# A pooled-attention and gated-MLP kernel: two softmax groups of the first batch move a product to GpSimd, PSUM tiles and the opening order are reassigned

## The chip, the cores and the metric

The kernel runs on one core of one Trainium2 chip. The metric is the device time of one execution, in microseconds (us), as the median of several runs. Smaller is better.

Five instruction streams work side by side: PE (TensorE, the matmuls; its weight loads are listed as PEld), DVE (VectorE), ACT (ScalarE), POOL (GpSimd) and SP (SyncE, which here issues nearly all DMAs). Each carries out its own instructions strictly in the order in which they were written; a wait of one instruction holds up everything behind it on that engine.

## The reference

Inputs are `q`, `k`, `v` of shape 8 batches x 8 heads x 576 positions x 64 features in float32, and the weights of a gated MLP; `w_in`, `w_sg` (float32) and `w_out` among them. `w_in` and `w_out` come as float64.

```python
k_p = k.reshape(B, H, 72, 8, 64).mean(axis=3)     # pool 576 keys to 72
v_p = v.reshape(B, H, 72, 8, 64).mean(axis=3)
scores = q @ k_p^T / 8;  scores -= max(scores)
attn = exp(scores);  attn = attn / (sum(attn) + 1e-9)
x = attn @ v_p                                    # 8 x 576 x 512
h = gelu(x @ w_in);  u, v = h[..., :512], h[..., 512:]
v_n = (v - mean(v)) / sqrt(var(v) + 1e-6) * g_ln
v_s = einsum('ts,bsd->btd', w_sg, v_n) + b_sg
out = x + (u * v_s) @ w_out
```

The product of the change is the division by the row sum: `attn / (sum + 1e-9)`, done as a multiplication by a reciprocal.

## The kernel before

One batch after another runs through the same steps, and the instructions of several batches are interleaved by hand. Every step is a Python generator that emits some instructions and stops at each `yield`; the piece between two yields is called a phase here. Two lists of tokens say in which order the phases are emitted: PROLOGUE once, then PERIOD for each batch. A token such as `S0+1` runs the next phase of step S for group 0 of batch 1; a lower-case token such as `v0` runs the next phase of a weight step, and `lv0` loads weights. At the end of the program every instruction gets a dependency on the one before it on its engine, so the order of the tokens is the order on every engine and on the DMA queue of SP.

The steps: A and B load keys and values (two loads each, 2 groups of heads at once), C loads queries, E loads the last 8 pooled rows' raw data ("left"), K pools the keys (for batch 0 with matmuls into PSUM, `pool8`; later with a DVE reduction) and builds the transposed, scaled `kbd`; its own three phases for K2 are the DVE reduction of the left rows into `lp`, the transposes on PE, and four copies on ACT. P does the same for the values. Q makes the transposed queries (batch 0 on PE and ACT, later on DVE). S computes scores and softmax of one pair of heads ("group", 0 to 3). L and T transpose the probabilities, V multiplies by the values and writes x and its split into a high and a low float32r part. H, U, W, O are the MLP: the normalised half, the gate half, the product with w_sg, the output product. Z stores. The weight steps v, u, o convert a quarter of w_in or w_out from float64 words in five phases (two ACT, two DVE, one POOL, one ACT, one POOL instruction); the steps s transpose w_sg.

Step S (line 426) of batch 0 takes a PSUM tile from `mtile()`, of later batches from `atile()` (line 428). The groups listed in SOFTMAX (line 75), that is groups 0 and 3 of batch 0 and all of batch 1, go one way ("mode 2"): the maximum on DVE (line 439), scores minus maximum on DVE from PSUM to the tile `e` in SBUF (line 449), one exp on ACT (line 451), the row sum on DVE (line 459), plus 1e-9 on POOL (line 461). All other groups have 10 pairs of ACT instructions that take exp with the bias and accumulate the sum (line 456). Then the reciprocal goes into unused columns of the PSUM tile of the scores, and DVE multiplies:

```python
rec = flat[:, 0:SLOT * NT].rearrange(...)[:, :, 2 * SP:2 * SP + 2]
nc.vector.reciprocal(rec, ssum)
nc.vector.tensor_tensor(e, e, rec..., op=ALU.mult)
```

The last phase copies the columns of the left rows to the tile `el` on POOL (line 475), which step L transposes.

PSUM has room for four such tiles of two banks. They form two rings of two: `mps` from `mtile()` (line 93) and `aps` from `atile()` (line 96). Each call takes the other tile of its ring, and the first instruction that writes it waits until every reader of its last content is done.

Of the kernel before, what the change touches and what calls it, by code (L numbers as in the profile page):

```python
# [33 lines left out]
o1 K1+2 T1+1 T1+1 o1 o1 o0 W3+0 V0+1 B1+2 o1 o0 W2+0 T2+1 o0 V1+1 W3+0 T2+1 o3 o3 T2+1 o2 W0+0 V2+1 o2 K2+2 B0+2 o2
V1+1 T3+1 W1+0 T3+1 o3 T3+1 V1+1 W0+0 V2+1 Q0+2 W2+0 V2+1 W3+0 K2+2 W0+0 K2+2 W1+0 V3+1 V3+1 S0+2 W1+0 W0+0 Q1+2 P1+2
W2+0 W1+0 o2 S1+2 W3+0 S0+2 C2+2 P0+2 S0+2 V0+1 S1+2 Q2+2 O1+0 S1+2 C3+2 O1+0 O1+0 O0+0 O0+0 o2 V3+1 V3+1 O2+0 S0+2
O0+0 S2+2 o3 Z0+0 O2+0 S2+2 P2+2 H2+1 o3 S1+2 O2+0 A0+3 S2+2 C0+3 Z1+0 H2+1 T0+2 S0+2 Q3+2 A1+3 Z0+0 V1+1
# [760 lines left out]
```

## Time and profile before

| | before |
|---|---|
| median of 3 runs | 576.03 us (572.07 to 578.5) |
| the profiled execution | 574.59 us |
| its span, first to last instruction | 572.8 us |
| PE busy | 552.7 us, 96% of the span |
| DVE, ACT, POOL busy | 71%, 61%, 39% |
| mean granted TensorE clock | 0.993 of full speed (2.4 GHz) |

The span is what the trace covers; the 1.8 us between it and the execution's time lie around it. PE's busy share is high from the third of 40 slices to the last, so idle time of the other engines is to be read together with what PE waits for. In a row of a timeline the columns are: start in us, duration in us, engine, line, operation, output tile <- input tiles, shapes, count of merged instructions, and in brackets the idle time of the engine just before and what ended it.

### The profile page before, as it was taken

Reading aid. Unit: us, or ns where it says so; the run is one execution under the profiler, and the core shown is the slowest. Engines: PE = TensorE matmul, PEld = TensorE weight load, DVE = VectorE, ACT = ScalarE, POOL = GpSimd, SP = SyncE. Lnnn points to the kernel's source line nnn. Section 1 sums busy time; section 2 is a strip of 40 time slices with the busy share of each in tenths; the row PEclk is TensorE's granted clock in tenths of the full one; section 3 lists DMA queues with packets and bytes.
Section 4 is the critical chain, followed back from the end, with each engine's and each line's share of the span. In section 5 each row is a group of like instructions: output and inputs, shape, how many; then the busy total and the mean of one; then the engine's idle time right before and its main releaser. Section 6 shows DMA issues by size and latency. Waiting matters only on the chain.

```text
span 572.8 us, 10342 instructions
## 1 busy us (share of the span) xinstructions
PE 552.7 (96%) x3793; PEld 522.3 (91%) x3793; DVE 406.6 (71%) x572; ACT 350.9 (61%) x985; POOL 222.3 (39%) x304
## 2 busy tenths in 40 slices
PE   4699999999999999999999999999999999999996
PEld 4678899988999999998999989999999989998996
DVE  2688999978568875878667785778667765344454
ACT  1889795977549755677647766498546775412320
POOL 3437755933153340703335331523316231433240
PEclk9799999999999999999999999999999999999999
DMA  8996263452513435153411625133440211021105
GB/s 215 319 270 153 59 151 93 95 105 57 97 33 78 69 73 104 38 104 69 93 31 47 113 57 108 48 77 48 95 79 1 44 22 21 1 42 22 21 1 84
DMA packets 161602, 46.34 MB, mean 81 GB/s; under 512 B 149072, under 2 KB 149072, under 8 KB 161552
## 3 DMA queue, kind: packets, MB, share of 16 engines
q1 hardware_dynamic: 156688, 45.10, 36.6%
q10 hardware_dynamic: 4864, 0.59, 0.6%
q8 instruction: 30, 0.49, 0.4%
q14 instruction: 20, 0.16, 0.1%
HBM read 36.23 MB, written 9.44 MB: 80 GB/s over the span
## 4 chain that ended last, share of the span: by engine, by line
PE 83%; DVE 7%; DMA 4%; SPq 3%; ACT 2%; issue 1%; POOL 0%; DVEq 0%; ACTq 0%; POOLq 0%
PE mps L100 66%; PE aps L100 13%; PE aps L135 3%; SPq L155 3%; DMA stage<-in_moe_w_sg 1%; DMA qraw<-in_q 1%; DMA kvraw<-in_k 1%; DVE bst L583 1%; DVE nmax L439 1%; DVE e L469 1%; DVE e L449 1%; ACT e L456 1%; DVE vp L324 1%; DVE vg L589 0%; DVE ssum L459 0%
## 5 line engine op out<-in xcount | busy, mean ns | idle before, releaser
L100 PE MATMUL mps<-xhl,wih 128*128 128x288 f32 x512 | 89.9, 298 | 0.0
L100 PE MATMUL mps<-wih,xhl 128*128 128x512 f32 x256 | 85.7, 401 | 0.1
L100 PEld LDWEIGHTS mps<-xhl,wih 128*128 128x128 f32 x512 | 75.8, 188 | 1.7 <-ACT u L616 0.2
L671 POOL TENSOR_TENSOR glo<-u,ghi 128x576 fp32r<-128x576 f32 x28 | 39.6, 1428 | 91.3 <-ACT ghi L669 91.2
L456 ACT ACTIVATE e<-aps,nmax 128x72 f32<-128x72 f32 x240 | 73.4, 354 | 2.6 <-DVE nmax L439 2.3
L100 PE MATMUL mps<-wsh,vhh 128*128 128x288 f32 x256 | 58.6, 300 | 0.0
L100 PEld LDWEIGHTS mps<-wih,xhl 128*128 128x128 f32 x256 | 48.1, 188 | 10.8 <-DVE x L710 0.3
L456 ACT ACTIVATION_READ_ACCUMULATOR e<-aps,nmax 128x1 f32 x240 | 57.4, 240 | 0.0
L100 PE MATMUL mps<-wsl,vhh 128*128 128x288 f32 x256 | 57.3, 295 | 0.0
L100 PE MATMUL mps<-wsh,vhl 128*128 128x288 f32 x256 | 57.3, 295 | 0.0
L100 PE MATMUL mps<-xhl,wil 128*128 128x288 f32 x256 | 55.0, 296 | 0.0
L100 PE MATMUL mps<-ghi,woh 128*128 128x288 f32 x240 | 54.0, 301 | 0.4 <-DVE u L639 0.4
L541 POOL TENSOR_TENSOR xhl<-x,xhl 128x576 fp32r<-128x576 f32 x32 | 45.3, 1430 | 21.7 <-ACT xhl L539 21.7
L589 DVE TENSOR_SCALAR vg<-vg,mv,rstd 128x512 f32<-128x512 f32 (+1 forms) x40 | 39.3, 984 | 19.2 <-POOL rstd L587 19.2
L100 PE MATMUL mps<-glo,woh 128*128 128x288 f32 x240 | 52.7, 295 | 0.0
L100 PE MATMUL mps<-ghi,wol 128*128 128x288 f32 x240 | 52.7, 295 | 0.0
L586 POOL TENSOR_TENSOR rstd<-mv,eps 128x1 f32<-128x1 f32 (+1 forms) x40 | 10.8, 269 | 107.9 <-DVE mv L584 98.5
L660 DVE SCALAR_TENSOR_TENSOR mps<-mps,gcol,bbc 128x576 f32<-128x576 f32 x28 | 23.1, 825 | 39.4 <-PE mps L100 39.3
L100 PE MATMUL mps<-wil,xhl 128*128 128x512 f32 x128 | 50.6, 395 | 0.0
L579 ACT ACTIVATE vg<-mps 128x512 f32<-128x512 f32 x32 | 19.2, 600 | 45.2 <-PE mps L100 44.9
L599 POOL TENSOR_TENSOR vhl<-vg,vhh 128x512 fp32r<-128x512 f32 x32 | 41.5, 1297 | 8.2 <-ACT vhh L597 8.2
L100 PEld LDWEIGHTS mps<-wsl,vhh 128*128 128x128 f32 x256 | 42.2, 188 | 0.0
(161 smaller groups left out, 1417.5 us busy)
## 6 DMA issues: line engine op xcount, KB each, us to landing
kvraw<-in_k SPq DMA_DIRECT2D x32, 256.0 KB
qraw<-in_q SPq DMA_DIRECT2D x112, 72.0 KB
out<-y SPq DMA_DIRECT2D x112, 72.0 KB
kvraw<-in_v SPq DMA_DIRECT2D x28, 256.0 KB
raw<-in_moe_w_in SPq DMA_DIRECT2D x4, 1024.0 KB
raw<-in_moe_w_out SPq DMA_DIRECT2D x2, 1024.0 KB
stage<-in_moe_w_sg SPq DMA_DIRECT2D x4, 288.0 KB
left<-in_k SPq DMA_DIRECT2D x16, 64.0 KB
```

What stands on the lines that cost most here:

```text
L100: nc.tensor.matmul(o, lhsT, rhs, start=start, stop=stop)
L135: nc.tensor.transpose(ps[:rows, i * P:(i + 1) * P], src(i), ident if i < NT - 1 else swap)
L155: queue.dma_start(o, i)
L324: nc.vector.tensor_reduce(out=o, in_=t.rearrange("p a (r d) -> p a d r", r=POOL), axis=AX.X, op=ALU.add)
L456: nc.scalar.activation(e[:, i, h], slots[i][:, h], AF.Exp, bias=nmax[:, i, h:h + 1], **acc)
L541: (nc.vector if b in LO_DVE else nc.gpsimd).tensor_tensor(xhl[:, 1, g], x32[:, g], xhl[:, 0, g].bitcast(F32), op=ALU.subtract)
L579: nc.scalar.activation(vg, o, AF.Gelu_apprx_tanh)
L586: nc.gpsimd.tensor_tensor(rstd, mv[:, 1:2], eps[:n, 1:2], op=ALU.add)
L589: nc.vector.tensor_scalar(vg, vg, mv[:, 0:1], rstd, op0=ALU.subtract, op1=ALU.mult)
L599: (nc.gpsimd if i < NT - 1 else nc.vector).tensor_tensor(lo, vg, hi.bitcast(F32), op=ALU.subtract)
L660: nc.vector.scalar_tensor_tensor(vs, vs, gcol[:, d:d + 1], bbc.rearrange("p (a n) -> p a n", a=2), op0=ALU.mult, op1=ALU.add)
L671: nc.gpsimd.tensor_tensor(glo[:, d], uf, ghi[:, d].bitcast(F32), op=ALU.subtract)
```

## The change

Four edits. (1) For groups 0 and 3 of batch 0 the reciprocal is written into `ssum` in SBUF, over the sums, and no longer into the PSUM tile (REC_SB). (2) For the same two groups the product by it is issued on POOL, as a phase of its own between the reciprocal and the copies to `el` (MUL_POOL); so PROLOGUE has one more token for each. (3) Eighteen steps, listed in SWAP, take their PSUM tile from the other ring: S0 and S1, Q0, Q2 and Q3, K0 to K2, T0, T2, V2, H4, U1 and W0 of batch 0, s2, and T0, T3 and L0 of batch 1. (4) PROLOGUE has a new order; it has the same tokens otherwise. PERIOD is as before.

```diff
 PROLOGUE = """
-A1+0 A0+0 K0+0 E0+0 K1+0 K0+0 K2+0 lv0 K1+0 v1 K2+0 K2+0 C0+0 Q0+0 Q0+0 v0 v1 C1+0 C2+0 v1 B1+0 Q1+0 C3+0 v0 S0+0 v0
-Q2+0 Q1+0 v1 S0+0 Q2+0 v0 lv1 S0+0 S0+0 S1+0 S1+0 B0+0 S0+0 v0 S1+0 S0+0 S0+0 Q3+0 S2+0 v1 S1+0 T0+0 Q3+0 S0+0 S2+0
-S3+0 v2 v2 P1+0 ls0 S3+0 P0+0 S3+0 S2+0 S3+0 S1+0 S2+0 T0+0 E0+1 A1+1 S3+0 P2+0 S3+0 A0+1 s4 S2+0 S3+0 v3 v3 K2+1
-T1+0 S3+0 v3 lu0 s3 T1+0 L0+0 s3 C0+1 L0+0 V1+0 C1+1 s3 s4 v2 lo0 V1+0 K1+1 v2 V0+0 v2 V0+0 v3 V1+0 T2+0 T2+0 T3+0 s4
-T3+0 s2 V0+0 K0+1 s1 s1 K2+1 s2 V2+0 lu1 K2+1 v3 s2 V3+0 u0 B0+1 V2+0 Q0+1 s1 u0 Q1+1 S0+1 V3+0 S0+1 u1 S0+1 S0+1
-S1+1 u0 V2+0 V3+0 S1+1 S1+1 u1 u0 u1 H0+0 S1+1 S0+1 S0+1 V2+0 H0+0 S1+1 u0 H2+0 u1 S1+1 s0 S0+1 u1 H2+0 H0+0 S1+1 s0
-T0+1 H3+0 u2 C2+1 H2+0 u3 s0 V1+0 u2 V3+0 H0+0 H2+0 H3+0 H0+0 u3 u3 U1+0 B1+1 V0+0 H2+0 Q2+1 C3+1 u2 u3 H4+0 P0+1
-P1+1 U1+0 u2 T0+1 S2+1 H0+0 u3 P2+1 S2+1 S0+1 Q3+1 H2+0 u2 H4+0 S1+1 T0+1 H1+0 o1 S3+1 H4+0 H4+0 A0+2 U0+0 S2+1 H1+0
...
+A0+0 lv0 K0+0 v0 A1+0 v1 K1+0 E0+0 v1 K2+0 C0+0 v1 K1+0 C1+0 K0+0 C2+0 C3+0 K2+0 v0 Q0+0 Q1+0 v1 v0 K2+0 Q0+0 v0 S0+0
+S0+0 B1+0 Q2+0 Q1+0 S1+0 v0 S0+0 S1+0 Q2+0 Q3+0 S0+0 Q3+0 S0+0 v1 lv1 S0+0 B0+0 ls0 S3+0 A1+1 S1+0 S2+0 S0+0 S3+0
+S3+0 S2+0 S0+0 S3+0 S3+0 v3 S1+0 S0+0 T0+0 S3+0 P1+0 S3+0 T1+0 S2+0 S2+0 E0+1 T1+0 S1+0 v3 T0+0 S3+0 P0+0 S3+0 A0+1
+v2 S2+0 s4 P2+0 s4 v2 s4 v3 lu0 s3 C0+1 L0+0 L0+0 C1+1 lo0 s3 V0+0 s3 V0+0 lu1 K1+1 V1+0 v2 v2 T2+0 K0+1 V1+0 s2 v2
+s2 V0+0 s2 T3+0 V1+0 K2+1 T2+0 v3 s1 V2+0 T3+0 s1 Q0+1 C2+1 V1+0 s1 K2+1 u0 V3+0 K2+1 V2+0 V3+0 u0 v3 u0 S0+1 u0 Q1+1
+u1 S0+1 V3+0 S1+1 V0+0 S0+1 S0+1 S1+1 C3+1 S1+1 u1 V2+0 u1 S1+1 H0+0 H2+0 S0+1 S0+1 H0+0 B0+1 H2+0 u0 u2 S1+1 H1+0
+H0+0 S1+1 u1 s0 S0+1 H0+0 u1 H0+0 V3+0 s0 u2 V2+0 H0+0 H1+0 H4+0 S1+1 T0+1 H4+0 H2+0 Q2+1 B1+1 u2 s0 Q3+1 u3 H4+0 u3
+u3 U1+0 T0+1 H4+0 u2 U1+0 S3+1 H2+0 T0+1 u3 H2+0 P0+1 S0+1 u3 o1 S3+1 P1+1 u2 H2+0 o0 P2+1 S3+1 H4+0 H3+0 S2+1 S1+1
+H3+0 H1+0 C1+2 S2+1 S2+1 H4+0 S3+1 A0+2 S2+1 H3+0 U3+0 U3+0 U0+0 S3+1 H4+0 S3+1 S2+1 H1+0 S2+1 H1+0 U2+0 P2+1 U0+0
+H1+0 H3+0 C0+2 S3+1 lo1 S2+1 S3+1 K0+2 P2+1 H3+0 U2+0 T1+1 S2+1 H3+0 H4+0 L0+1 lb0 o1 L0+1 P2+1 A1+2 E0+2 W2+0 o1
...
@@ -74,6 +74,9 @@
     WHOLE = (0,)
     SOFTMAX = ((0, 0), (0, 3), (1, 0), (1, 1), (1, 2), (1, 3))
     ROUND = ()
+    REC_SB = ((0, 0), (0, 3))
+    MUL_POOL = ((0, 0), (0, 3))
+    SWAP = ("H4.0", "K0.0", "K1.0", "K2.0", "L0.1", "Q0.0", "Q2.0", "Q3.0", "S0.0", "S1.0", "T0.0", "T0.1", "T2.0", "T3.1", "U1.0", "V2.0", "W0.0", "s2",)
     LO_W = ()
     W_POOL = ()
 
@@ -90,11 +93,18 @@
         turns[name] = (turns.get(name, -1) + 1) % bufs
         return pool.tile(shape, F32, name=name, tag=f"{name}{turns[name]}")
 
+    doing = [""]
+
+    def either(first):
+        if first != (doing[0] in SWAP):
+            return ring(psm, [P, 2, NB], "mps", 2)
+        return ring(psa, [P, 2, NB], "aps", 2)
+
     def mtile():
-        return ring(psm, [P, 2, NB], "mps", 2)
+        return either(True)
 
     def atile():
-        return ring(psa, [P, 2, NB], "aps", 2)
+        return either(False)
 
     def mm(o, lhsT, rhs, start, stop):
         nc.tensor.matmul(o, lhsT, rhs, start=start, stop=stop)
@@ -464,9 +474,14 @@
             yield
             nc.vector.tensor_scalar(ssum, ssum, 1e-9, None, op0=ALU.add)
 
-        rec = flat[:, 0:SLOT * NT].rearrange("p (s k) -> p s k", k=SLOT)[:, :, 2 * SP:2 * SP + 2]
+        if (b, g) in REC_SB:
+            rec = ssum
+        else:
+            rec = flat[:, 0:SLOT * NT].rearrange("p (s k) -> p s k", k=SLOT)[:, :, 2 * SP:2 * SP + 2]
         nc.vector.reciprocal(rec, ssum)
-        nc.vector.tensor_tensor(e, e, rec.unsqueeze(3).broadcast_to([P, NT, 2, SP]), op=ALU.mult)
+        if (b, g) in MUL_POOL:
+            yield
+        (nc.gpsimd if (b, g) in MUL_POOL else nc.vector).tensor_tensor(e, e, rec.unsqueeze(3).broadcast_to([P, NT, 2, SP]), op=ALU.mult)
         ef = st["e", b, g] = e.rearrange("p t h k -> p t (h k)")
         yield
         if ("el", b) not in st:
@@ -738,6 +753,7 @@
         if 0 <= b < B:
             if (name, b) not in going:
                 going[name, b] = steps[name[0]](b, int(name[1]))
+            doing[0] = f"{name}.{b}"
             next(going[name, b], None)
 
     def weight(name):
@@ -750,6 +766,7 @@
             else:
                 load_w(name[1], i)
         else:
+            doing[0] = name
             if name not in going:
                 going[name] = (step_s if name[0] == "s" else step_w)(name[0], int(name[1]))
             next(going[name], None)
```

## Rows read from the trace of the kernel before

**Rows 1.** The page: busy time of the engines, share of the span, instructions.

```profile
PE 552.7 (96%) x3793; PEld 522.3 (91%) x3793; DVE 406.6 (71%) x572; ACT 350.9 (61%) x985; POOL 222.3 (39%) x304
```

**Rows 2.** Stretches of the span: from:to, length, busy time and instructions of PE, PEld, DVE, ACT, POOL, then granted TensorE clock (1 is 2.4 GHz), DMA share, GB/s.

```profile
0.00:10.00 10.00, 1.87 (x9) 1.90 (x10) 2.72 (x3) 1.28 (x1) 5.65 (x22) 1.00 0.66 199
10.00:20.00 10.00, 8.75 (x67) 8.17 (x67) 4.67 (x7) 5.90 (x14) 2.53 (x2) 1.00 1.22 271
20.00:30.00 10.00, 6.68 (x36) 6.52 (x35) 6.58 (x12) 8.15 (x40) 4.58 (x9) 0.66 0.98 340
30.00:40.00 10.00, 9.00 (x62) 7.32 (x61) 9.31 (x13) 8.39 (x20) 3.64 (x7) 1.00 0.94 234
50.00:87.00 37.00, 36.20 (x230) 32.16 (x229) 36.32 (x56) 31.06 (x52) 24.71 (x37) 1.00 0.47 109
87.00:556.00 469.00, 468.43 (x3257) 447.03 (x3257) 331.21 (x460) 285.52 (x841) 173.18 (x222) 1.00 0.31 60
```

**Rows 3.** The timeline of PE: the pooling and transposes of the keys, the score products of batch 0, the first product with the values, the transposes of batch 1's keys, its score products, and the first product of step H.

```profile
13.76 0.27 PE L345 MATMUL aps<-ident,kp 128*128 128x128 f32 x1
14.45 0.27 PE L347 MATMUL aps<-ident,lp 128*128 128x128 f32 x1
16.90 1.49 PE L100 MATMUL mps<-kbd,qT 128*128 128x144 f32 x10 [0.98 <-ACT qT L418]
23.96 2.74 PE L100 MATMUL mps<-kbd,qT 128*128 128x144 f32 x10 [3.32 <-DVE e L469]
36.91 0.65 PE L100 MATMUL aps<-ah,vb 128*128 128x288 f32 x2
44.31 0.44 PE L345 MATMUL aps<-ident,kp 128*128 128x128 f32 x2
44.69 0.65 PE L100 MATMUL aps<-ah,vb 128*128 128x288 f32 x2
48.59 2.62 PE L100 MATMUL aps<-kbd,qT 128*128 128x144 f32 x20
50.95 0.49 PE L100 MATMUL mps<-wih,xhl 128*128 128x512 f32 x1
```

**Rows 4.** The timeline of ACT between 14 and 38 us: the weight conversion's two instructions, the first and last of the 20 exp instructions of S1 and the first of S2, exp of a mode-2 group, and the copies of the steps T, P2, L0 and s4.

```profile
14.12 0.68 ACT L196 ACTIVATE top<-raw 128x512 f32<-128x512 f32 x1
14.70 0.68 ACT L200 ACTIVATE raw<-raw 128x512 int32<-128x512 uint32 x1
21.31 0.30 ACT L456 ACTIVATE e<-mps,nmax 128x72 f32<-128x72 f32 x1
24.27 0.69 ACT L418 COPY qT<-aps 128x576 f32<-128x576 f32 x1
27.85 0.32 ACT L456 ACTIVATE e<-mps,nmax 128x72 f32<-128x72 f32 x1 [1.77 <-PE aps L135]
31.75 0.80 ACT L451 ACTIVATE e<-e 128x720 f32<-128x720 f32 x1 [0.77 <-DVE e L449]
32.47 0.62 ACT L507 COPY ah<-aps 128x576 f32<-128x576 f32 x1
33.44 0.77 ACT L390 ACTIVATE vb<-aps 64x256 f32<-64x256 f32 x2 [0.35 <-PE aps L100]
37.10 1.28 ACT L486 COPY lt<-aps 32x576 f32<-32x576 f32 x2
38.41 1.27 ACT L240 CAST wth<-mps 64x576 fp32r<-64x576 f32 x2
```

**Rows 5.** The timeline of DVE: the reduction of the left rows for batch 0, the two instructions of a weight conversion, the softmax of group 0 (maximum, difference, sum, product), a reduction for batch 1's keys, and the low part of a quarter of w_sg.

```profile
9.17 1.90 DVE L324 TENSOR_REDUCE lp<-left 64x128 f32<-64x1024 f32 x1 [5.92 <-DMA left<-in_v]
14.83 0.43 DVE L202 TENSOR_SCALAR top<-top 128x512 int32<-128x512 int32 x1 [3.76 <-ACT top L196]
18.52 0.90 DVE L439 TENSOR_REDUCE nmax<-mps 128x10 f32<-128x720 f32 x1
19.46 0.91 DVE L449 TENSOR_TENSOR e<-mps,nmax 128x720 f32<-128x720 f32 x1
22.91 0.90 DVE L469 TENSOR_TENSOR e<-e,mps 128x720 f32<-128x720 f32 x1
41.74 1.98 DVE L324 TENSOR_REDUCE kp<-kvraw 128x128 f32<-128x1024 f32 x1
45.63 0.76 DVE L160 TENSOR_TENSOR wsl<-mps,wsh 128x576 fp32r<-128x576 f32 x1 [1.90 <-ACT wsh L158]
```

**Rows 6.** Groups of POOL instructions by shape: busy time, mean ns of one, idle before them.

```profile
L541 POOL TENSOR_TENSOR xhl<-x,xhl 128x576 fp32r<-128x576 f32 x32 | 45.3, 1430 | 21.7 <-ACT xhl L539 21.7
L599 POOL TENSOR_TENSOR vhl<-vg,vhh 128x512 fp32r<-128x512 f32 x32 | 41.5, 1297 | 8.2 <-ACT vhh L597 8.2
```

**Rows 7.** One DVE instruction of the normalisation in a later batch, twice, and the POOL instruction that was running at the second one's start.

```profile
190.82 0.55 DVE L589 TENSOR_SCALAR vg<-vg,mv,rstd 128x512 f32<-128x512 f32 x1 [0.94 <-POOL rstd L587]
...
193.46 1.27 DVE L589 TENSOR_SCALAR vg<-vg,mv,rstd 128x512 f32<-128x512 f32 x1
...
193.16 1.29 POOL L599 TENSOR_TENSOR vhl<-vg,vhh 128x512 fp32r<-128x512 f32 x1
```

**Rows 8.** The DMA queue of SP, timeline: start and duration of issuing, tiles, count; keys 256 KB each, left 64 KB each, w_in 1024 KB.

```profile
0.73 2.62 SPq L155 DMA_DIRECT2D kvraw<-in_k  x4
6.44 0.44 SPq L155 DMA_DIRECT2D raw<-in_moe_w_in  x1
```

More of the change, by code (lines that the diff above doesn't have):

```diff
@@ L29 @@
-S1+1 u0 V2+0 V3+0 S1+1 S1+1 u1 u0 u1 H0+0 S1+1 S0+1 S0+1 V2+0 H0+0 S1+1 u0 H2+0 u1 S1+1 s0 S0+1 u1 H2+0 H0+0 S1+1 s0
-T0+1 H3+0 u2 C2+1 H2+0 u3 s0 V1+0 u2 V3+0 H0+0 H2+0 H3+0 H0+0 u3 u3 U1+0 B1+1 V0+0 H2+0 Q2+1 C3+1 u2 u3 H4+0 P0+1
-P1+1 U1+0 u2 T0+1 S2+1 H0+0 u3 P2+1 S2+1 S0+1 Q3+1 H2+0 u2 H4+0 S1+1 T0+1 H1+0 o1 S3+1 H4+0 H4+0 A0+2 U0+0 S2+1 H1+0
-H4+0 S3+1 S2+1 H1+0 U3+0 S3+1 o0 S3+1 H3+0 lo1 U0+0 H4+0 C0+2 S2+1 H3+0 S3+1 S2+1 S3+1 U2+0 H1+0 S2+1 H3+0 S3+1 H4+0
-H3+0 K0+2 P2+1 P2+1 A1+2 P2+1 lb0 S2+1 H1+0 S3+1 U3+0 H4+0 C1+2 H1+0 L0+1 T1+1 L0+1 L0+1 U2+0 L0+1 W2+0 o0 V0+1 E0+2
@@ L34 @@
[L34 to L37, printed above, removed]
+A0+0 lv0 K0+0 v0 A1+0 v1 K1+0 E0+0 v1 K2+0 C0+0 v1 K1+0 C1+0 K0+0 C2+0 C3+0 K2+0 v0 Q0+0 Q1+0 v1 v0 K2+0 Q0+0 v0 S0+0
@@ new lines @@
+H0+0 S1+1 u1 s0 S0+1 H0+0 u1 H0+0 V3+0 s0 u2 V2+0 H0+0 H1+0 H4+0 S1+1 T0+1 H4+0 H2+0 Q2+1 B1+1 u2 s0 Q3+1 u3 H4+0 u3
+u3 U1+0 T0+1 H4+0 u2 U1+0 S3+1 H2+0 T0+1 u3 H2+0 P0+1 S0+1 u3 o1 S3+1 P1+1 u2 H2+0 o0 P2+1 S3+1 H4+0 H3+0 S2+1 S1+1
+H3+0 H1+0 C1+2 S2+1 S2+1 H4+0 S3+1 A0+2 S2+1 H3+0 U3+0 U3+0 U0+0 S3+1 H4+0 S3+1 S2+1 H1+0 S2+1 H1+0 U2+0 P2+1 U0+0
+H1+0 H3+0 C0+2 S3+1 lo1 S2+1 S3+1 K0+2 P2+1 H3+0 U2+0 T1+1 S2+1 H3+0 H4+0 L0+1 lb0 o1 L0+1 P2+1 A1+2 E0+2 W2+0 o1
+L0+1 V0+1 L0+1 o1 T1+1 o1 o0 T1+1 W3+0 o3 W2+0 o0 o0 V0+1 o0 V1+1 T2+1 o3 V0+1 V1+1 o2 W3+0 K2+2 T2+1 o3 o2 T2+1 o2
@@ L38 @@
+o3 K1+2 Q0+2 W3+0 T3+1 W0+0 W2+0 V2+1 W1+0 W0+0 T3+1 V1+1 V2+1 W0+0 T3+1 Q1+2 K2+2 W1+0 B0+2 K2+2 V3+1 V1+1 B1+2 W3+0
+P1+2 S0+2 V3+1 W0+0 W2+0 W1+0 C2+2 W1+0 S1+2 S1+2 O0+0 O0+0 S0+2 O1+0 V2+1 Q2+2 o2 O1+0 V3+1 O0+0 S0+2 P0+2 S0+2 o2
+O2+0 C3+2 Z0+0 S2+2 O1+0 C0+3 O2+0 S2+2 S1+2 o3 P2+2 H2+1 S1+2 S0+2 O2+0 S2+2 T0+2 H2+1 Z0+0 A1+3 V3+1 Q3+2 Z1+0 A0+3
 """.split()
```

## The prediction

> **What bounds the kernel now.** I read the page's busy times first, then a table of stretches, then the timeline of PE, and only where PE waits the timelines of the engine it waits for. PE is busy for 552.7 us of the span [rows 1]. The stretches say where the other 20 us are: from 87 to 556 us PE idles for 0.6 us and from 50 to 87 us for 0.8 us, so in this part every matmul delays the end and no other engine matters as long as it stays ahead of PE [rows 2]. PERIOD isn't touched, and the change adds or removes no matmul. What it can move is therefore what PE loses before about 50 us, and any new waits in the part of PROLOGUE that runs until about 160 us.
>
> The losses before 50 us are of three kinds. PE starts its first work near 8 us, when the first keys have landed. From 8 to about 17 us it pools and transposes keys, paced by DMAs, ACT and DVE; the first score product (S0) starts at 16.90 [rows 3]. Then the third score product starts at 23.96, after 3.32 us of idle time that a DVE product (line 469) ended: the tile of S0 holds the reciprocal until that product at 22.91 to 23.81 has read it [rows 3, 5]. Behind that idle stretch the granted clock falls: its mean is 0.66 from 20 to 30 us, against 1.00 around it [rows 2], which is a spell at the 1.2 GHz level, and ten matmuls of the third product take 2.74 us where the first ten took 1.49 [rows 3].
>
> What is PE waiting for afterwards? The first product with the values starts at 36.91, and its second half needs `lt`, which ACT begins to write at 37.10 [rows 3, 4]. ACT is busy 8.15 and 8.39 us in the two stretches of 10 us before that [rows 2], so at most 3.5 us can be squeezed out of ACT's list between 20 and 40 us, however quickly PE runs. This is my bound on what the removed PE stall is worth: the stall itself and the slow clock (up to (1 - 0.66) x 10 = 3.4 us) sum to 6.7 us, but ACT, one engine further, lets only part of that through.
>
> **Part 1: reciprocals in SBUF.** The tile of S0 becomes free after the subtraction (19.46 + 0.91 = 20.37) and not after the product (23.81): 3.4 us earlier [rows 5]. S3's likewise. On ACT the gain is the 1.77 us that it waited for S2's scores at 27.85 and the 0.77 us before S3's exp [rows 4]. The price of the reciprocal itself is nil: same instruction, another address.
>
> **Part 2: products on POOL.** DVE loses two instructions of 0.90 us [rows 5]. POOL's row for two inputs is 1.297 us at 512 columns and 1.430 at 576 [rows 6], so 2.1 ns per column and 1.73 us at 720; the operand repeated along a row isn't shown on POOL. Bounds: 0.90 us (as DVE) to 3.5 us (twice); I take 1.73, since the shape is near those rows. The path of group 0 becomes 0.83 us longer. It is hidden by S1's 20 exp instructions on ACT (21.31 to 24.27) and by S3's and S2's products on PE; at 3.5 us it would push T0, and T1 behind it on PE, by nearly 2 us, of which T1's own wait for S1's product (a DVE instruction behind S3's sum) hides about 1.
>
> DVE and POOL can block each other: the same tensor_scalar takes 0.55 us alone and 1.27 us when it starts 0.30 us after a POOL instruction of 1.29 us, ending 0.28 us after it [rows 7]. The new products stand at about 23 to 25 and 29 to 31 us, where DVE reads PSUM maxima and differences, with one SBUF input at most; a small tensor_scalar of S2 may wait a few tenths of a us. I add nothing for it. The Trainium skill, page "SBUF — State Buffer", section "Who interferes with whom", has it as a rule: the port pair that the two share is held for a whole instruction, and a DVE instruction with two SBUF inputs also blocks with a POOL one that reads SBUF. It speaks against part 2; by it a product could cost DVE up to its own length, so the sum would be about 1 us worse.
>
> **Part 3: rings and order at the start.** The queue was keys 1, keys 0, left, w_in; now it is keys 0, w_in (1024 KB), keys 1, left. The two conversions v0 and v1 now stand ahead of the pooled keys' copies on ACT (each 14.12 to 15.38, 1.26 us), and the first conversion's two DVE instructions (0.43 + about 0.7) ahead of the reduction of the left rows (1.90) [rows 4, 5]. The landing of w_in isn't shown; keys 0 and w_in are 1.57 MB, which at 271 and 199 GB/s [rows 2] from about 2 us on (four key loads take 2.62 us to issue from 0.73 on, w_in one of 0.44 us [rows 8]) are there at 7.8 and 9.9 us. With 2.6 us on ACT, 1.1 and 1.9 on DVE, the reduction ends between 13.4 and 15.5. From its transpose to S0 took 2.45 us (14.45 to 16.90) [rows 3]. So S0 starts between 15.9 and 18.0 instead of 16.90; I take 17.3, nearer the late end because keys 1 too now wait for w_in: 0.4 us later. In exchange v0 and v1 are done by then, 2.6 us of ACT work that stood among the softmax work before.
>
> **Part 4: from S0 to the first product with the values.** Following ACT in its new order: S1's 20 instructions start near 22.3 and take 2.96 us (21.31 to 24.27), 0.5 us of waiting for S3's difference, S3's exp 0.80, a conversion 1.26, S2's 20 instructions 2.96, two T copies 1.24, a conversion 1.26, `vb` 0.77 and `wth` 1.27 [rows 4]. That sum is 35.3 to 35.6 for the first copy of `lt`, against 37.10: about 1.5 us earlier. PE has its work before that done by 35 us (T0, T1, both value poolings, s4, s3, L0), as before the change.
>
> **Part 5: to step H.** From the first value product at 36.91 to step H at 50.95 PE ran for 14.0 us almost without waiting [rows 3]; the same matmuls follow now. One wait is new: DVE's reductions for batch 1 (two of 1.95, the left rows' 1.95) now stand in a block behind the low part of s3, and the transposes that need them come after V2 and no longer before it. DVE reaches the block at 38.3 and ends at 38.3 + 1.95 + 1.95 + 0.75 + 1.95 = 44.9 [rows 5], against 44.31 for these transposes before [rows 3]. PE has V2 behind it at 44.7, so it waits only some 0.3 us. Behind it come V3 and two score products, (50.95 - 48.59) + 1.95 = 4.3 us, with about 0.3 for the queries that DVE transposes in between: step H near 49.8, 1.1 us earlier than 50.95.
>
> **Part 6: H to the period.** From 50 to 87 us DVE is busy 36.32 of 37 us and PE 36.20 [rows 2]: both are full, and both now start about 1.1 us earlier with the same work. I let the new order there cost nothing net.
>
> **The sum**, against the profiled execution's 574.6 us: 0.4 later, 1.9 gained on ACT, 0.4 lost before step H, so -1.1 us: 573.5. The median of the three runs is 1.4 us above that execution; the same gain from the median is 574.9.
>
> **Rivals.** (a) *The PE stall is all that counted*: PE then gains the 3.3 us and the 3.4 us of slow clock, 567.9 us. For it: it is the one long wait in PE's timeline and the only stretch of these with a lower clock [rows 2]. Against it: ACT's 8.15 and 8.39 of 10 us. (b) *The keys come late*: keys 1 and the left rows wait for 1.05 MB of weights, 3.1 us at 340 and 3.9 us at 271 GB/s [rows 2], and this reaches S0 in full. At 3.9 us later instead of 0.4 the sum is 574.6 - 1.1 + 3.5 = 577.0, slower than before. It decides from S0 at 18.4 on. Against it: in the old order PE needed both key loads and pooled them from 8 to 13.9 us, so half of that pooling now runs during w_in's transfer. (c) *DVE falls behind*: between 50 and 87 us DVE has no slack, so each DVE instruction that now stands ahead of one that PE awaits, such as line 398's ahead of the last softmax product of batch 1, delays PE by its length; six of the size of the product's 0.90 us [rows 5] are 5.4 us less the 1.1, 578.9 us. I found one such place and PE's later matmuls could hide part of it. (d) *Nothing happens*: the stall only moves to the next wait, 574.6.
>
> **How the numbers follow.** One per cent is 5.8 us, about what a measurement of this kernel can tell from no change; faster means under 570.3, slower over 581.8. My forecast with (d), 571 to 576: 0.50. (a), with anything under 570.3: 0.22. (b): 0.14, all within 1%. (c) and waits of the new order that I didn't see: 0.14, most of it over 578 and 0.10 over 581.8. So faster 0.22, same 0.68, slower 0.10. The range leaves out a tenth on either side: from rival (a)'s 568 to 580, which takes in (b) and (c)'s mean and the median's 1.4 us.
>
> **What would show it.** Right: in the changed trace S3 or S2 starts by 22 to 24 us with no wait for a product, the mean granted clock of 20 to 30 us is 0.8 or more, POOL's two products take about 1.7 us, the first `lt` copy starts at 35 to 36 us and step H at 49 to 50.5. Wrong: S0 after 18.4 (then (b)); `lt` before 33 (then ACT wasn't the bound, (a)); waits of PE for DVE between 50 and 87 us of more than 2 us in sum (then (c)). A time under 568 would mean that step H's start moved by more than ACT's list allows.

## The result and the profile after

The changed kernel is 0.9% slower: 581.01 us (median of 11 runs, 576.93 to 582.28) against 575.68 us for the kernel before beside it, ratio 1.0092 with a 95% interval of 1.0066 to 1.0119. The profiled execution took 579.32 us with a span of 577.4 us, against 574.59 and 572.8 before.

The page, beside [rows 1]: PE is busy for 1.2 us more though the matmuls are the same, and DVE for 3.4 us more with two instructions fewer.

```profile
PE 553.9 (96%) x3793; PEld 522.7 (91%) x3793; DVE 410.0 (71%) x570; ACT 350.8 (61%) x985; POOL 227.1 (39%) x306
```

The stretches of the changed kernel, columns as in [rows 2]; the last two run from the first product of step H to the first of step O, and from there on.

```profile
10.00:20.00 10.00, 7.05 (x50) 6.61 (x51) 4.81 (x6) 6.09 (x15) 3.95 (x4) 0.83 0.88 211
20.00:30.00 10.00, 7.61 (x64) 7.08 (x63) 7.96 (x13) 8.88 (x41) 4.16 (x9) 1.00 0.93 310
50.00:87.00 37.00, 34.76 (x220) 30.68 (x218) 35.73 (x55) 29.15 (x48) 24.80 (x36) 1.00 0.49 119
100.00:110.00 10.00, 9.20 (x57) 9.01 (x58) 8.71 (x11) 5.83 (x13) 6.92 (x5) 0.83 0.58 112
48.95:111.20 62.25, 56.97 (x372) 52.23 (x371) 59.11 (x78) 45.11 (x77) 40.03 (x48) 0.97 0.45 104
111.20:577.00 465.80, 460.93 (x3196) 439.31 (x3194) 319.01 (x453) 271.41 (x815) 160.49 (x213) 1.00 0.31 59
```

The same two stretches of the kernel before:

```profile
50.95:106.79 55.84, 54.95 (x372) 50.58 (x371) 54.80 (x78) 44.20 (x76) 37.39 (x47) 1.00 0.44 100
106.79:572.00 465.21, 460.69 (x3196) 439.06 (x3194) 320.12 (x454) 272.22 (x817) 161.28 (x214) 1.00 0.31 60
```

Both have the same 372 matmuls and 78 DVE instructions between H and O, but the changed kernel takes 62.25 us for them instead of 55.84, **6.4 us more**. PE's idle time there grew from 0.9 to 5.3 us, and DVE's busy time by 4.3 us. In this pair of executions H starts 2.0 us earlier, and behind O the difference is 0.2 us.

The timeline of PE in the changed kernel, beside [rows 3]: the pooling of the second key load, the lines of [rows 3], and every wait over 0.4 us between H and O:

```profile
11.73 3.12 PE L110 MATMUL mps<-kvraw,apart 128*128 128x128 f32 x16 [3.23 <-DMA kvraw<-in_k]
17.81 1.49 PE L110 MATMUL aps<-kbd,qT 128*128 128x144 f32 x10 [0.69 <-ACT qT L428]
22.61 2.72 PE L110 MATMUL mps<-kbd,qT 128*128 128x144 f32 x20 [1.05 <-ACT qT L428]
43.96 0.38 PE L355 MATMUL aps<-ident,kp 128*128 128x128 f32 x2
48.95 0.49 PE L110 MATMUL mps<-wih,xhl 128*128 128x512 f32 x1
...
76.72 0.81 PE L110 MATMUL mps<-xhl,wih 128*128 128x288 f32 x4 [0.96 <-ACT u L631]
80.62 0.66 PE L145 MATMUL aps<-ident,e 128*128 128x128 f32 x4 [0.43 <-DVE e L484]
82.17 0.63 PE L145 MATMUL mps<-ident,el 128*64 128x128 f32 x4 [0.78 <-POOL el L490]
100.80 0.40 PE L110 MATMUL aps<-ah,vbh 128*128 128x288 f32 x1 [3.04 <-DVE al L528]
111.20 0.52 PE L110 MATMUL mps<-ghi,woh 128*128 128x288 f32 x2
```

With keys 0 alone PE starts at 4.75 us instead of 8.13, but then waits 3.23 us for keys 1, and a spell of the slower clock now lies between 10 and 20 us (mean 0.83, 1.00 before) and no longer between 20 and 30. The largest new wait behind H is 3.04 us, for `al` of V2+1, a DVE result. Behind it the granted clock has a spell at the 1.2 GHz level (mean 0.83 from 100 to 110 us). What held DVE up is seen in the timelines of DVE and then POOL in the changed kernel, from 86 us on: the conversion of w_out (lines 212 and 213 on DVE, 215 and 220 on POOL; 202, 203, 205 and 210 before) and what stands beside it.

```profile
87.72 0.43 DVE L212 TENSOR_SCALAR top<-top 128x512 int32<-128x512 int32 x1
88.19 1.69 DVE L213 SCALAR_TENSOR_TENSOR top<-raw,top 128x512 int32<-128x512 int32 x1
89.91 0.76 DVE L528 TENSOR_TENSOR al<-aps,ah 128x576 fp32r<-128x576 f32 x1
...
92.11 1.47 DVE L212 TENSOR_SCALAR top<-top 128x512 int32<-128x512 int32 x1
93.61 1.80 DVE L213 SCALAR_TENSOR_TENSOR top<-raw,top 128x512 int32<-128x512 int32 x1
...
100.00 0.75 DVE L528 TENSOR_TENSOR al<-aps,ah 128x576 fp32r<-128x576 f32 x1
```

```profile
88.03 1.30 POOL L220 TENSOR_TENSOR wol<-top,woh 128x512 fp32r<-128x512 f32 x1 [0.73 <-ACT woh L218]
89.95 1.33 POOL L215 TENSOR_TENSOR top<-top,raw 128x512 int32<-128x512 int32 x1 [0.63 <-DVE top L213]
92.01 1.28 POOL L220 TENSOR_TENSOR wol<-top,woh 128x512 fp32r<-128x512 f32 x1 [0.73 <-ACT woh L218]
93.25 1.61 POOL L556 TENSOR_TENSOR xhl<-x,xhl 128x576 fp32r<-128x576 f32 x1
```

Each of these three DVE conversion instructions starts while a POOL subtraction with SBUF operands runs, and ends only after it: 88.19 + 1.69 is 0.55 us after 88.03 + 1.30, and likewise at 92.11 and 93.61. The difference at line 528, which has one operand in PSUM, keeps its 0.76 us beside POOL's addition at 89.95. In the kernel before, o0 and o1 were converted on DVE one behind the other, and POOL started when both were done (timelines of DVE and POOL before):

```profile
87.43 0.69 DVE L203 SCALAR_TENSOR_TENSOR top<-raw,top 128x512 int32<-128x512 int32 x1
88.50 0.69 DVE L203 SCALAR_TENSOR_TENSOR top<-raw,top 128x512 int32<-128x512 int32 x1
89.27 2.59 POOL L205 TENSOR_TENSOR top<-top,raw 128x512 int32<-128x512 int32 x2 [5.89 <-DVE top L203]
```

Three instructions of 1.69, 1.47 and 1.80 us for their 0.69, 0.43 and 0.69 are 3.2 us; the tensor_scalar of [rows 7] had shown the same lock.

That gives **theory L**: the new order of the back half lets DVE and POOL shut each other out, PE waits for what DVE then has late, and the clock falls behind the wait. Its rivals: the front of the change costs the time; the order of DVE's work as such does (T2+1's difference too late, say); POOL's own time does.

### The profile page after: what moved, and what is told of

Read it like the earlier page. It is cut to its first block, busy times and chain, and to the rows that moved or that the text cites. A ratio compares the mean times of both kernels' runs of the same rounds, so it can differ in the third digit from the quotient of the medians.

```text
span 577.4 us, 10340 instructions
## 1 busy us (share of the span) xinstructions
PE 553.9 (96%) x3793; PEld 522.7 (91%) x3793; DVE 410.0 (71%) x570; ACT 350.8 (61%) x985; POOL 227.1 (39%) x306
## 4 chain that ended last, share of the span: by engine, by line
PE 83%; DVE 9%; ACT 3%; issue 2%; DMA 1%; POOL 1%; SPq 0%; DVEq 0%; POOLq 0%
PE mps L110 66%; PE aps L110 13%; PE aps L145 3%; DMA kvraw<-in_k 1%; DVE nmax L449 1%; ACT e L466 1%; DVE e L459 1%; DVE top L212 1%; DVE bst L598 1%; DVE vg L604 1%; DVE top L213 1%; DVE e L484 0%; DVE vp L334 0%; SPq L165 0%; DVE al L528 0%
## 5 line engine op out<-in xcount | busy, mean ns | idle before, releaser
L110 PE MATMUL mps<-xhl,wih 128*128 128x288 f32 x496 | 87.1, 298 | 1.0 <-ACT u L631 1.0
L466 ACT ACTIVATE e<-aps,nmax 128x72 f32<-128x72 f32 x250 | 76.3, 351 | 1.3 <-DVE nmax L449 1.0
L110 PEld LDWEIGHTS mps<-xhl,wih 128*128 128x128 f32 x496 | 73.5, 189 | 2.5 <-ACT u L631 1.2
L466 ACT ACTIVATION_READ_ACCUMULATOR e<-aps,nmax 128x1 f32 x250 | 59.4, 238 | 0.0
L110 PE MATMUL mps<-wsh,vhh 128*128 128x288 f32 x248 | 57.3, 302 | 0.0
L110 PE MATMUL mps<-wsl,vhh 128*128 128x288 f32 x248 | 56.0, 297 | 0.0
L110 PE MATMUL mps<-wsh,vhl 128*128 128x288 f32 x248 | 56.0, 297 | 0.0
L604 DVE TENSOR_SCALAR vg<-vg,mv,rstd 128x512 f32<-128x512 f32 (+1 forms) x40 | 40.5, 1012 | 19.6 <-POOL rstd L602 19.6
L110 PE MATMUL mps<-xhl,wil 128*128 128x288 f32 x248 | 53.3, 296 | 0.0
L110 PE MATMUL aps<-kbd,qT 128*128 128x144 f32 x300 | 41.0, 287 | 1.1 <-ACT qT L428 0.7
```

The lines of the kernel that those rows point to most:

```text
L110: nc.tensor.matmul(o, lhsT, rhs, start=start, stop=stop)
L466: nc.scalar.activation(e[:, i, h], slots[i][:, h], AF.Exp, bias=nmax[:, i, h:h + 1], **acc)
L604: nc.vector.tensor_scalar(vg, vg, mv[:, 0:1], rstd, op0=ALU.subtract, op1=ALU.mult)
```

## The experiments

Each line of results gives the median, the ratio to the kernel before on the same chip with its 95% interval, and "H to O", the time between the first products of these steps in the profiled run (55.84 us before, 62.25 us after).

**Which half: the new front alone (e1_new_front), the new back alone (e2_new_back).** The order, SWAP and, for e2, REC_SB and MUL_POOL are mixed from the two kernels, split shortly ahead of step H.

```diff
 PROLOGUE (e1: from "u1 S1+1" on as before)
-u1 S0+1 V3+0 S1+1 V0+0 S0+1 S0+1 S1+1 C3+1 S1+1 u1 V2+0 u1 S1+1 H0+0 H2+0 S0+1 S0+1 H0+0 B0+1 H2+0 u0 u2 S1+1 H1+0
+u1 S0+1 V3+0 S1+1 V0+0 S0+1 S0+1 S1+1 C3+1 S1+1 u1 V2+0 u1 S1+1 B0+1 H0+0 S0+1 S0+1 V2+0 H0+0 S1+1 u0 H2+0 u1 S1+1 s0
...
 PROLOGUE (e2: to there as before), and in e2
-    REC_SB = ((0, 0), (0, 3))
-    MUL_POOL = ((0, 0), (0, 3))
+    REC_SB = ()
+    MUL_POOL = ()
```

> The changed kernel with its new order, rings and POOL products up to the first token of step H, and from there on the remaining tokens in the order of before, with the rings of before. Theory D (the back half of the new PROLOGUE costs the time: there DVE's difference for step T of batch 1, group 2, comes too late for PE, and other waits with it): step H starts near 49 us as in the changed kernel, no wait of PE above 0.5 us behind it, span 570.8, ratio to before 0.9965. Rival F (the front causes it: the POOL products and the moved conversions push work of DVE and ACT into the part behind, whatever its order): waits of PE between 60 and 105 us stay, ratio 1.003 or more.

> The order, rings and DVE products of before up to step H, and from there on the remaining tokens in the new order with the new rings of those steps. Theory D: the 6.4 us that the changed kernel lost between the start of step H and the first product of step O are lost here too, span near 579, ratio 1.011, with a wait of some 3 us for line 528's difference. Rival F: ratio 0.998 to 1.003.

e1: 574.78 us, 0.9986 (0.9961 to 1.0012), H to O 56.10 us and no wait over 0.4 us behind H. e2: 581.88 us, 1.0111 (1.0083 to 1.0140), H to O 63.30 us, with the same wait in its timeline of PE:

```profile
100.46 0.61 PE L110 MATMUL aps<-ah,vbh 128*128 128x288 f32 x1 [3.03 <-DVE al L528]
```

The whole loss sits in the back half, its order and rings together; the front is no slower than before, and not measurably faster. In this run of e2 the old front reached step H at 48.79 us, as early as the new front in the run of the changed kernel (48.95) and 2.2 us earlier than in the run of the kernel before (50.95). One execution's start of H therefore says little about the front.

**One token: T2+1's difference ahead of K2+2's reduction (e3_t2_early).**

```diff
-... o3 V0+1 V1+1 o2 W3+0 K2+2 T2+1 o3 o2 T2+1 o2
+... o3 V0+1 V1+1 o2 W3+0 T2+1 T2+1 K2+2 o3 o2 o2
```

> The changed kernel with one token moved: the third phase of T for group 2 of batch 1 (DVE's difference) right behind its second phase, ahead of the reduction of the left rows of batch 2 and two conversion phases. Theory D: the wait of 3.0 us and the 3.4 us at the slow clock behind it go, 4.5 to 5 us, span 572.5, ratio to before 1.000. Rival D2 (DVE is simply late with everything): the wait moves to the transposes of the keys of batch 2, which need the reduction put back; 1 to 2 us are gained, ratio 1.006. Rival F: no gain.

579.77 us, 1.0077 (1.0053 to 1.0101), H to O 60.37 us; the ratio can't be told from the changed kernel's. The wait moved to the next result that DVE has late (timeline of PE):

```profile
108.33 0.41 PE L355 MATMUL aps<-ident,kp 128*128 128x128 f32 x2 [2.37 <-DVE u L677]
```

DVE as a whole is behind; it is not one instruction that stands too late.

**The front's edits singly: reciprocals in SBUF alone (e4_rec_only), with the products on POOL in the old order (e7_rec_pool), the change with its products on DVE (e6_products_dve).**

```diff
 e4 and e7, against the kernel before:
-        rec = flat[:, 0:SLOT * NT].rearrange(...)[:, :, 2 * SP:2 * SP + 2]
+        rec = ssum if (b, g) in ((0, 0), (0, 3)) else flat[:, 0:SLOT * NT].rearrange(...)[:, :, 2 * SP:2 * SP + 2]
 e7 also (and one more token for each of the two groups in PROLOGUE):
-        nc.vector.tensor_tensor(e, e, rec.unsqueeze(3).broadcast_to([P, NT, 2, SP]), op=ALU.mult)
+        if (b, g) in ((0, 0), (0, 3)):
+            yield
+        (nc.gpsimd if (b, g) in ((0, 0), (0, 3)) else nc.vector).tensor_tensor(e, e, ..., op=ALU.mult)
 e6, against the changed kernel:
-    MUL_POOL = ((0, 0), (0, 3))
+    MUL_POOL = ()
```

> The kernel before with one edit: the reciprocals of groups 0 and 3 of batch 0 in SBUF; products still on DVE, order and rings of before. As predicted (ACT is the bound behind the PE wait): the third score product starts by 21 us, the first copy of lt 1.5 to 2 us earlier than 37.10, ratio 0.997. Rival (the PE wait and the slow clock are all that counted): 5 to 6.7 us gained, ratio 0.990. Rival (nothing moves): 1.000.

> The kernel before with the reciprocals of groups 0 and 3 of batch 0 in SBUF and their products on POOL, order and rings of before (the product's phase right behind the reciprocal). Parts 1 and 2 of the change alone. As predicted: ratio 0.996 to 0.998, as with the reciprocals alone or 0.3 us different. If products on POOL are what costs: 1.003 or more.

> The changed kernel with the two products back on DVE, reciprocals still in SBUF. If moving the products to POOL is worth something: DVE has 1.8 us more between 23 and 31 us, step H starts up to 0.9 us later, ratio 1.009 to 1.011. If the products on POOL cost (rival: they hold DVE up): ratio 1.006 or less. The waits of PE between 75 and 101 us are the same in both.

e4: 572.91 us, 0.9982 (0.9952 to 1.0011). The stall is gone, and a smaller wait follows (timeline of PE):

```profile
20.88 1.42 PE L100 MATMUL mps<-kbd,qT 128*128 128x144 f32 x10
23.84 0.63 PE L135 MATMUL aps<-ident,e 128*128 128x128 f32 x4 [1.54 <-DVE ssum L465]
```

From S0 to H it takes 32.98 us (15.99 to 48.97) instead of 34.05, so at most 1.1 us of the 3.3 us of stall came through in this pair of executions. Even that isn't shown to come from the edit: e2, whose front is that of the kernel before, took 32.35 us from S0 to H (16.44 to 48.79), and there PE waited only 1.50 us for the product. e7 missed its expectation: 577.94 us, 1.0037 (1.0008 to 1.0066). In the old order PE waits for the product on POOL, and then for S1's on DVE (timeline of PE):

```profile
28.76 0.66 PE L135 MATMUL aps<-ident,e 128*128 128x128 f32 x4 [2.12 <-POOL e L471]
31.30 2.74 PE L100 MATMUL mps<-kbd,qT 128*128 128x144 f32 x10 [1.77 <-DVE e L471]
```

e6: 580.96 us, 1.0101 (1.0067 to 1.0135), and 31.33 us from S0 to H against 31.14 in the changed kernel (31.13 to 31.17 in e5, e9, e11 and e13, which like these two run S0 at the full clock). By these traces the products on POOL are worth about 0.2 us in the new order, which the ratios can't show; in the old order the kernel with them (e7) is slower than the kernel before.

**Two more of the front: group 1 in mode 2 as well, with its phases spread over the order (e8_third_mode2, on e1), and the old tokens up to S0 (e10_old_start, on e1).**

```diff
 e8:
-    SOFTMAX = ((0, 0), (0, 3), (1, 0), ...)
-    REC_SB = ((0, 0), (0, 3))
+    SOFTMAX = ((0, 0), (0, 1), (0, 3), (1, 0), ...)
+    REC_SB = ((0, 0), (0, 1), (0, 3))
 e10:
-A0+0 lv0 K0+0 v0 A1+0 v1 K1+0 E0+0 v1 K2+0 C0+0 v1 K1+0 C1+0 K0+0 C2+0 C3+0 K2+0 v0 Q0+0 Q1+0 v1 v0 K2+0 Q0+0 v0 S0+0
+A1+0 A0+0 K0+0 E0+0 K1+0 K0+0 K2+0 lv0 K1+0 v1 K2+0 K2+0 C0+0 Q0+0 Q0+0 v0 v1 C1+0 C2+0 v1 B1+0 Q1+0 C3+0 v0 S0+0 v1
 ...
```

> The front of the changed kernel and the back of before (as in the first of these runs), and group 1 of batch 0 too takes its softmax the way of groups 0 and 3: ten pairs of ACT instructions, 2.96 us, become one of 0.8 us, DVE gets 1.6 us more. If ACT sets the first product with the values: lt and step H start 1.5 to 2 us earlier relative to the first score product than in the first run, ratio to before 0.995. If DVE or the DMAs set it: no change, ratio 0.998 to 1.000.

> The tokens of before up to the first score product, from there the new order up to step H, and the order of before behind that; rings, reciprocals in SBUF and products on POOL as in the first run. If the new DMA order is what makes the first score product late (17.6 to 19.9 us in the runs with it, 16.0 to 19.2 in those without): it starts near 17, step H 31 to 32 us behind it, ratio to before 0.994 to 0.997. If the start makes no difference: ratio as in the first run, 0.9985.

e8: 575.42 us, 1.0005 (0.9985 to 1.0024): less work on ACT gained nothing, so ACT isn't the only bound there; PE then waited 1.62 us for DVE at T0. e10: 574.97 us, 0.9987 (0.9957 to 1.0017), missing what I expected; S0 came at 18.30, behind waits of 2.57 and 0.69 us for DMAs.

**Theory L, one collision: V0+1's low part of x on POOL (93.25, 1.61) moved behind the last difference of T2+1 (e5_xlo_late).**

```diff
-... V1+1 T2+1 o3 V0+1 V1+1 o2 W3+0 K2+2 T2+1 o3 o2 T2+1 o2
+... V1+1 T2+1 o3 V1+1 o2 W3+0 K2+2 T2+1 o3 o2 T2+1 V0+1 o2
```

> The changed kernel with one token moved: the POOL phase of V for group 0 of batch 1 (the low part of x) goes from ahead of DVE's phase for o3 and o2 to behind DVE's difference of T for group 2. The order on DVE is the same as in the changed kernel. Theory L (DVE is late because POOL holds it: the scalar_tensor_tensor of o3's conversion took 1.80 us behind that POOL instruction instead of 0.69): it takes 0.7 us, the difference for T ends 1.1 us earlier than 100.76 relative to step H, PE's wait there falls from 3.0 to about 2 us, ratio to before 1.006 to 1.0075. Rival O (only the order on DVE counts): wait and ratio stay, 1.009.

579.33 us, 1.0085 (1.0052 to 1.0117), H to O 61.22 us. o3's instruction takes 0.69 us instead of 1.80, and PE waits 1.0 us less (timelines of DVE and PE):

```profile
94.79 0.69 DVE L213 SCALAR_TENSOR_TENSOR top<-raw,top 128x512 int32<-128x512 int32 x1
```

```profile
100.97 0.45 PE L110 MATMUL aps<-ah,vbh 128*128 128x288 f32 x1 [2.04 <-DVE al L528]
```

The trace shows the microsecond that theory L asks for; the ratio alone could not have told it from the changed kernel's.

**Theory L, the other collisions: POOL's low parts of w_out over 16 of 512 columns (e9_short_wol, on e5), then with POOL as long busy there without reading (e13_memset_wol).**

```diff
+    nc.gpsimd.memset(wol.bitcast(F32), 0.0)
...
+            if name == "o":
+                nc.gpsimd.memset(lo[:, :, 4:].bitcast(F32), 0.0)
+                nc.gpsimd.memset(lo[:, :, 4:].bitcast(F32), 0.0)
+                lo, top, hi = lo[:, :, 0:4], top[:, :, 0:4], hi[:, :, 0:4]
```

The first line and the shortening to 0:4 are in both runs, the two fills in e13 alone; both also have e5's moved token.

> The changed kernel with the POOL phase of V for group 0 of batch 1 moved back as in the fifth run, and POOL's low parts of w_out taken over 16 columns of each quarter's 512 only (the rest of that low part is zero: part of the computation is left out). Order on DVE and PE as in the changed kernel. Theory L (POOL's instructions hold DVE's conversions up): no tensor_scalar or scalar_tensor_tensor of a conversion above 0.9 us from 86 us on, DVE 3 us less busy there, PE's wait for the difference of T below 0.5 us, no spell of the slow clock, and from step H to the first product of step O 57 to 58.5 us instead of 62.25; ratio to before 1.000 to 1.002. Rival O (the order of DVE's work alone): 1.0 us better than the changed kernel at most, as in the fifth run, ratio 1.007.

> The run with w_out's low parts over 16 columns (e9_short_wol), but GpSimd fills the 496 columns left out with zeros, twice, ahead of each low part: at the 0.52 us of the 128x512 fills in the trace it is busy about 1.27 us there again, as with the whole low part (1.30), yet it reads nothing of SBUF. The output still lacks those columns of w_out's low parts. Theory L (VectorE is shut out while GpSimd reads): VectorE's conversions stay 0.4 and 0.7 us, 57 to 58.3 us from step H to step O, ratio 0.996 to 1.002. If it is GpSimd's own time there that made the loss: the conversions stay short, but low parts and what waits for them come late, 59.5 us or more from H to O, ratio 1.003 or more. If a fill shuts VectorE out too: the conversions beside a fill are 1.1 us or longer, and H to O is 60 us or more.

e9: 575.56 us, 0.9988 (0.9961 to 1.0015), H to O 57.43 us; the wait at V2+1 is gone, with the spell at 1.2 GHz behind it. Its stretch from H to O, columns as in [rows 2]:

```profile
48.93:106.36 57.43, 55.38 (x373) 50.70 (x371) 56.07 (x78) 45.00 (x78) 37.37 (x48) 1.00 0.45 109
```

e13: 576.05 us, 1.0014 (0.9988 to 1.0040), H to O 57.45 us. The timelines of DVE and POOL in e13:

```profile
87.94 0.43 DVE L213 TENSOR_SCALAR top<-top 128x512 int32<-128x512 int32 x1
88.41 0.69 DVE L214 SCALAR_TENSOR_TENSOR top<-raw,top 128x512 int32<-128x512 int32 x1
91.33 0.47 DVE L213 TENSOR_SCALAR top<-top 128x512 int32<-128x512 int32 x1
91.83 0.69 DVE L214 SCALAR_TENSOR_TENSOR top<-raw,top 128x512 int32<-128x512 int32 x1
```

```profile
87.46 0.51 POOL L222 MEMSET wol<- 128x496 f32 x1
88.02 0.80 POOL L223 MEMSET wol<- 128x496 f32 x1
88.79 0.39 POOL L225 TENSOR_TENSOR wol<-top,woh 128x16 fp32r<-128x16 f32 x1
91.01 0.51 POOL L223 MEMSET wol<- 128x496 f32 x1
```

POOL is busy from 87.46 to 89.18, longer than the 1.30 us of the whole low part, and PE loses nothing against e9. So what cost these microseconds was POOL's reading beside DVE; POOL's own time did not matter.

**Two attempts at a complete kernel: conversions in pairs by seven tokens (e11_paired), and in the manner of the kernel before (e12_reversed).** The back segment of e12:

```diff
-... lb0 o1 L0+1 P2+1 A1+2 E0+2 W2+0 o1
-L0+1 V0+1 L0+1 o1 T1+1 o1 o0 T1+1 W3+0 o3 W2+0 o0 o0 V0+1 o0 V1+1 T2+1 o3 V0+1 V1+1 o2 W3+0 K2+2 T2+1 o3 o2 T2+1 o2
+... lb0 L0+1 P2+1 A1+2 E0+2 W2+0 T1+1 L0+1
+V0+1 L0+1 o0 o1 o1 o0 T1+1 W3+0 V0+1 W2+0 o1 o0 o1 o0 V1+1 T2+1 V0+1 V1+1 W3+0 T2+1 K2+2 T2+1 o3 o3 o2 o2 o2 o3 K1+2
 ...
```

> The changed kernel, complete, with seven tokens of its back half moved so that DVE's instructions with two SBUF inputs meet no running POOL instruction: the conversion phases of o0 and o1 on DVE stand together, ahead of POOL's, those of o3 and o2 together behind the reduction of the left rows of batch 2, the POOL phase of V for group 0 of batch 1 and DVE's difference of T for group 2 as in the fifth and third run. Theory L: conversions on DVE at 0.4 and 0.7 us, no wait of PE above 1 us between 84 and 106 us, no slow clock there, 57 to 58.5 us from step H to the first product of step O instead of 62.25, ratio to before 0.998 to 1.001. If the order on DVE were the cause and POOL were not: a wait of 1.5 us or more stays for the transposes of the keys of batch 2, ratio 1.005 or more.

> The changed kernel, complete, with the back half's conversions set in pairs: VectorE converts o0 and o1 one behind the other (and o3 beside o2), GpSimd starts only when both are converted and takes o1 (o2) first; V0+1's low part of x goes right behind o0's on GpSimd, and P2+1's last VectorE phase, T1+1's copy and T2+1's difference come earlier. Theory L (the loss is VectorE and GpSimd shutting each other out): VectorE's conversion instructions from 86 us on are 0.4 and 0.7 us long as before the change, no PE wait over 1 us between 84 and 106 us, 56.5 to 58.5 us from step H to step O instead of 62.25, and a ratio of 0.998 to 1.001. If the loss is in the order of VectorE's work as such: the short instructions come back, but the waits and the ratio (1.005 or more) stay.

e11: 582.76 us, 1.0139 (1.0097 to 1.0181), H to O 64.64 us, the slowest of all and a miss for theory L's numbers. POOL took o1 while DVE still had o0 to convert, so the collision came back (timelines of POOL and DVE), and again at 102.11 (1.68 us):

```profile
86.01 1.40 POOL L215 TENSOR_TENSOR top<-top,raw 128x512 int32<-128x512 int32 x1 [2.90 <-DVE top L213]
```

```profile
86.30 1.66 DVE L213 SCALAR_TENSOR_TENSOR top<-raw,top 128x512 int32<-128x512 int32 x1
```

PE waited 2.11 us at 88.79 and 3.64 us at 107.97, the latter for the transposes of batch 2's keys, as the rival had it. With the collisions back the run doesn't separate the two; but DVE also stood idle there (2.48 us for ACT before 97.77), so the order costs time in it beside the lock.

e12: 580.76 us, 1.0101 (1.0059 to 1.0143), H to O 60.89 us: a miss for theory L's numbers on H to O and on the ratio, which came out as the rival had it. Its conversions take 0.42 to 0.69 us (one tensor_scalar, at 100.53, took 1.35), and no PE wait between 84 and 106 us exceeds 1 us, as theory L expected. But the two additions of POOL now stand behind both conversions, and ACT waits for them (timelines of ACT and PE):

```profile
95.66 0.64 ACT L553 COPY x<-aps 128x576 f32<-128x576 f32 x1 [3.89 <-POOL top L215]
```

```profile
80.40 0.80 PE L110 MATMUL mps<-xhl,wih 128*128 128x288 f32 x4 [1.04 <-ACT u L631]
98.64 0.53 PE L110 MATMUL aps<-wsh,vhh 128*128 128x288 f32 x2 [0.97 <-ACT x L553]
```

From H to O PE idles 5.1 us in small waits (60.89 - 55.77, from the table of stretches), nearly as much as the 5.3 us of the changed kernel. So e12 doesn't speak against theory L as the cause in the changed kernel's own order, where e5, e9 and e13 have it; it shows that another order, almost without the lock, can lose nearly as much to ACT. No run gives a complete kernel that measurably beats the kernel before; e4 (0.9982), e1 (0.9986) and e10 (0.9987) come nearest.

## Why the prediction was wrong

The median, 581.01 us, lies 1.0 us above the upper end of the range. The sum missed the profiled execution by 5.8 us (573.5 against 579.32): step H came 0.85 us earlier than forecast, the stretch from H to O took 6.41 us more than it was given, and the stretch behind O 0.2 us more.

- **Part 6 failed**: "I let the new order there cost nothing net." The prediction had DVE full there (36.32 of 37 us), but put at nothing what the new order does to DVE's instructions; from H to O it cost 6.4 us. e2, which has this part alone, is slower by 1.11%. Of the 6.4 us, 1.0 come back when one collision is taken away (e5: 62.25 to 61.22) and another 3.8 with the others (e9: 57.43). Those 4.8 us include the slower clock behind the long wait: V2+1's eight matmuls and the first w_sg product take 1.80 and 4.63 us there, 1.08 and 3.76 at 91.64 and 87.88 of the same trace, 1.6 us in all. The last 1.6 us (57.43 against 55.84) are left when the lock is gone. They come with the new order and rings of the back half, which no run separates, and stand mostly in the waits at 76.72, 80.62 and 82.17, of which e9 still has 0.65, 0.44 and 0.78 us.
- **Part 2's lock was weighed in the wrong place.** The rows showed it [rows 7], and it was asked only of the two new products, where "I add nothing for it" was harmless: beside the first of them DVE's maximum takes its 0.91 us, and beside the second DVE has nothing to do. The same lock between moved instructions, 60 us later, decided. The Trainium skill, page "SBUF — State Buffer", section "Who interferes with whom", states it for a DVE instruction with two SBUF inputs: this trace agrees (0.69 us became 1.69 and 1.80), and the difference with a PSUM operand was left alone at 0.76.
- **Rival (c)** named the engine, the direction and by luck the size (578.9 against 579.32), with a chance of 0.14. Its mechanism was another, instructions standing ahead of others rather than growing longer, and its test looked between 50 and 87 us, where PE waits only 0.43 us for DVE; the wait came at 100.80. The reading that behind 87 us "no other engine matters as long as it stays ahead of PE" was right, but in the new order DVE did not stay ahead.
- **Parts 1 to 5 came out in the profiled execution, in part by luck.** The third score product starts at 22.61 with no wait for a softmax product, and the mean clock from 20 to 30 us is 1.00. POOL's product took 1.39 us, under the 1.73 taken. S0 at 17.81 lies within the 15.9 to 18.0 given, though in other runs with the new start it was as late as 20.42. ACT in the changed kernel and in e2, then POOL in the changed kernel:

```profile
34.98 1.28 ACT L501 COPY lt<-aps 32x576 f32<-32x576 f32 x2
```

```profile
34.95 1.28 ACT L501 COPY lt<-aps 32x576 f32<-32x576 f32 x2
```

```profile
23.64 1.39 POOL L484 TENSOR_TENSOR e<-e,ssum 128x720 f32<-128x720 f32 x1 [0.39 <-DVE ssum L481]
```

  `lt` at 34.98 answers the 35.3 to 35.6 forecast, the transposes of batch 1's keys came at 43.96 without the 0.3 us of waiting, and H at 48.95 for 49.8. But e2, with the old front and its reciprocals in PSUM, had `lt` at 34.95 and H at 48.79, and no slow clock between 20 and 30 us. In the eight profiled runs with the complete new front `lt` began between 34.75 and 38.61 us and H between 48.69 and 52.58. So the agreement of one execution doesn't show that the front earns what parts 1 to 5 give it. Whether it is worth its 1.1 us isn't settled by times either: e1 measured 0.8 us less than before (0.14% of 574.3), with an interval from 2.2 less to 0.7 more.
- **Rivals (a), (b) and (d).** (a) is out: 567.9 us would be a ratio of 0.988, and the intervals of e4, with the stall gone, and of e1 begin at 0.9952 and 0.9961. (b) was right that keys 1 come late: in the ten profiled runs with the new start PE waited 1.71 to 4.43 us for them, and in four S0 was past its 18.4 us. It did not decide the time: e1, with the new start, is no slower than before (0.9986), and the old start (e10) gained nothing over the new one. (d) fits e4 and e1 within their intervals as well as my sum does.
